# Attention and a mixture of experts on one core: joins and id copies on VectorE, earlier jump hints, a bank for the last tile, row stores one by one

## The chip, the core and the metric

The kernel runs on one core of one Trainium2 chip. The core has five engines that run side by side, each with an instruction stream of its own: TensorE (PE in the profile; its weight loads are PEld), VectorE (DVE), ScalarE (ACT), GpSimd (POOL) and SyncE (SP, which only issues transfers). The metric is the device time of one execution in microseconds (us).

## The reference

Windowed attention (8 batches, 8 heads, 576 positions, head size 64; each position sees itself and the 63 before it) gives 4608 tokens of 512 numbers. Each token goes to one of 8 experts, the one with the largest gate logit:

```python
logits = x @ w_gate
e_idx = np.argmax(logits, axis=1)
...
gate_w = probs[np.arange(N), e_idx]
eom = 1.0 / (1.0 + np.exp(-(x @ w_output_gate)))
for e in range(E):
    mask = e_idx == e
    h = np.maximum(x[mask] @ w1[e], 0.0)
    ye = h @ w2[e]
    out[mask] = gate_w[mask, None] * eom[mask, e, None] * ye
```

Everything is in 32-bit floats; w1 is 512 x 1024 and w2 is 1024 x 512 for each expert.

## The kernel before, in words

**Attention.** The loop over `t` takes 36 tiles of 128 tokens. For each it computes scores, exponentials, transposes and the product with v, and GpSimd copies the result (`xb`) into a row tile `xr` (L278), split into upper and lower halves of each 32-bit word. Tokens are routed in groups of four tiles (`GROUPS`; the last three groups are smaller). `route_a` finds each token's expert and weight, `route_b` its row in the buffer `xs` in device memory, which has a region for each expert; then it stores the rows with one indirect transfer for each tile of the group, all at once (L391 to L394, GpSimd's queue). A row holds the 512 words, the token's id and its weight. `xr` has two buffers. Early rows of expert 0 (two tiles) are read back while attention still runs (`early`, from group 6 on) and go through `joined` and `split` at L544.

**Experts.** `load_tile` (L483, L484) reads 128 rows by a transposing transfer into `halves`, and their ids and weights into `info`; both are issued by SyncE. `joined` puts the words together again from the two halves: GpSimd copies the upper half (L489), VectorE the lower (L490). `split` makes two parts, `xhi` on ScalarE (L493) and the rest `xlo` on VectorE (L494), so that three fast matmuls stand for one of full precision. `prep` calls both for two or four tiles. `layer1` runs 8 blocks of 12 matmuls into three banks of `ps_1`; ScalarE and VectorE evict each block as `hhi` and `hlo` (L623, L624). `layer2` runs 24 matmuls for one tile of 128 tokens into a bank of `ps_y` (three banks), VectorE evicts it times the weight into `y` (L639), and GpSimd stores it row by row by its ids (L640). `layer2_half` does a tile with at most 64 tokens; for it, GpSimd moves part of `hlo` into `hhi` (L627).

While an expert's layer 1 runs, `piece` splits the weights of the next one: ScalarE copies the upper part (L109), VectorE and GpSimd subtract (L110), and ScalarE's queue issues the load of a later piece into the `raw` buffer that has come free (L97).

**Order.** How many tokens an expert has is known only at run time. A Switch (L756) with 26 arms for each expert jumps to the code that fits: one pass of up to 512 columns, or one of 256 or 512 and a last one. All five engines jump. Each reads the number of the arm from memory into a register (`held`, L571) and gets a hint (`switch_hint`), so that the code of the arm is fetched ahead. Before, load and hint for the next expert stand after the arms (L779, L780), ahead of the last tile, `layer2(ws, 1, last)` (L781). As the program is built, each arm begins with a hint to its own end. A pass goes `masked` or a copy of the ids (L744), loads for the next pass, `layer1`, `prep`, then layer-2 tiles 2, 3 and 0; tile 1 comes last. In the section of the experts the order of TensorE, ScalarE and VectorE is as written (`manual_schedule`, L711); the order of GpSimd's and SyncE's instructions, and of all engines in the attention loop, is chosen by the compiler's scheduler. The data give experts 0, 1, 3 and 5 one pass and experts 2, 4, 6 and 7 two.

Of the kernel before, what the change touches and what calls it, by code (L numbers as in the profile page):

```python
# [19 lines left out]
P = 128  # L20
# [3 lines left out]
DM = H * D  # L24
# [16 lines left out]
def attn_moe(ctx: ExitStack, tc: tile.TileContext, qT, kT, vp, wg, w1, w2, out):  # L41
# [78 lines left out]
    ac = pool(rest, "ac", 1)  # L120
    erow = ac.tile([P, 8, 2 * P], U16, name="erow")
    nc.gpsimd.memset(erow, 0)
    xbp, xrp, xtp, gsp, sm = pool(rest, "xbp", 2), pool(rest, "xrp", 2), pool(rest, "xtp", 2), pool(rest, "gsp", 2), pool(rest, "sm", 4)
    ps_g = pool(rest, "ps_g", 1, space=PSUM)
    qsp, ktp, vpl = pool(big, "qsp", 3), pool(big, "ktp", 3), pool(big, "vpl", 3)
    pp, ptp = pool(big, "pp", 4), pool(big, "ptp", 2)
# [210 lines left out]
                                axis=AX.X, op=ALU.add)  # L337

    rts = {}

    def route_a(gi):

# [28 lines left out]
    def route_b(gi):  # L371

        G, (lg, _), xr = GROUPS[gi], bank_of(gi), xrs[gi]
        ohb, wm, ssum = rts.pop(gi)
        rk = lg[:, :, 2 * NE:3 * NE]
        for j in range(G):
            nc.tensor.matmul(rk[:, j], ones, ebase, start=True, stop=False)
            nc.tensor.matmul(rk[:, j], ones, csum_b, start=False, stop=False)
            for jj in range(j):
                nc.tensor.matmul(rk[:, j], ones, ohb[:, jj], start=False, stop=False)  # L380
            nc.tensor.matmul(rk[:, j], tri, ohb[:, j], start=False, stop=True)

        nc.vector.scalar_tensor_tensor(out=ssum, in0=wm, scalar=1.0, in1=ssum, op0=ALU.add, op1=ALU.mult)
        nc.vector.reciprocal(out=xr[:, 0:G, DM + 1:DM + 2].bitcast(F32), in_=ssum.unsqueeze(2))
        de = sm.tile([P, 4, NE], F32, name="de")[:, 0:G]
        nc.vector.tensor_tensor(out=de, in0=rk[:, 0:G], in1=ohb, op=ALU.mult)
        df = sm.tile([P, 4], F32, name="df")
        nc.vector.tensor_reduce(out=df[:, 0:G], in_=de, axis=AX.X, op=ALU.add)
        di = sm.tile([P, 4], I32, name="di")
        nc.vector.tensor_copy(out=di[:, 0:G], in_=df[:, 0:G])  # L390
        for j in range(G):  # L391
            ins = nc.gpsimd.indirect_dma_start(
                out=xs[:, :], out_offset=bass.IndirectOffsetOnAxis(ap=di[:, j:j + 1], axis=0),
                in_=xr[:, j, :], in_offset=None)  # L394

            tc.declare_no_dep(ins.ins, group="rows", reason="each token has a row of its own")
            tc.add_to_no_dep_group("rows", ins.ins)
        if gi == len(GROUPS) - 1:
            totals(ohb)
            return  # L400

        cs = sm.tile([P, NE], F32, name="cs")
        nc.vector.tensor_reduce(out=cs, in_=ohb.rearrange("p g e -> p e g"), axis=AX.X, op=ALU.add)
        nc.vector.tensor_tensor(out=csum, in0=csum, in1=cs, op=ALU.add)
        nc.vector.tensor_copy(out=csum_b, in_=csum)
# [80 lines left out]
    def joined(halves, x):  # L486

        words = x.bitcast(U16).rearrange("p k (n w) -> p k w n", w=2)
        nc.gpsimd.tensor_copy(out=words[:, :, 1], in_=halves[:, 0:KC])  # L489
        nc.vector.tensor_copy(out=words[:, :, 0], in_=halves[:, KC:2 * KC])  # L490

    def split(x, hi, lo):
        nc.scalar.copy(hi, x)  # L493
# [12 lines left out]
    for t in range(NT):  # L506
        if t + 4 < NT and t % 2 == 0:
            load_qk(t + 4)
            load_v(t + 4)
        if t % 3 == 1 and t // 3 < NPC:  # L510
            raws.append(load_piece(0, t // 3, nc.sync))
        if t % 3 == 0 and t > 0 and t // 3 <= NPC:
            split_piece(wsets[0], t // 3 - 1, raws.pop(0), nc.gpsimd.tensor_copy, (nc.gpsimd, nc.gpsimd))
        if 28 <= t < 26 + NRAW:
            load_piece(1, t - 28, nc.sync)
        if t < NT:
            ptrans(t)
        if t + 1 < NT:
            expo(t + 1, 0)
        for args in pend_s:  # L520
            gate_sum(*args)
        if t + 2 < NT:
            scores(t + 2)
        for gi in pend_b:
            route_b(gi)
            if gi == EARLY:
                early()
        pend_b = []
        for gi, gj, _ in pend_s:
            if gj + 2 == GROUPS[gi]:  # L530
                route_a(gi)
                pend_b.append(gi)
        pend_s = []
        if 1 <= t <= NT:
            xtrans(t - 1)
        if t >= NT - 2:
            i = t - (NT - 2)
            if i == 0:
                ehi = wst.tile([P, KC, 2 * P], F32R, name=f"raw{NRAW - 2}")
                elo = wst.tile([P, KC, 2 * P], F32R, name=f"raw{NRAW - 1}")  # L540
            cs = slice(i * P, (i + 1) * P)
            xe = xbp.tile([P, DM], F32, name="xb")
            xe = xe.rearrange("p (k n) -> p k n", k=KC)
            joined(erow[:, :, cs], xe)  # L544
            split(xe, ehi[:, :, cs], elo[:, :, cs])
        if t + 1 < NT:
            expo(t + 1, 1)
        if t < NT:
            pv(t)
        if 1 <= t <= NT:  # L550
            gi, gj = place[t - 1]
            if GROUPS[gi] < 4:
                gate_one(t - 1)
                if gj == GROUPS[gi] - 1:
                    route_a(gi)
                    pend_b.append(gi)
            elif gj % 2 == 1:
                pend_s.append(gate_pair(t - 1))
# [68 lines left out]
                nc.gpsimd.tensor_copy(out=hhi[f][:, half + 64:half + P], in_=hlo[f][:, half:half + 64])  # L627
            between(f)

    def layer2(ws, i, cur):  # L630
        yp = ps_y.tile([P, DM], F32, name="yp")
        cs = slice(i * P, (i + 1) * P)
        for f in range(FC):
            wh, wl = ws['h2'][f // 2][:, f % 2, :], ws['l2'][f // 2][:, f % 2, :]
            nc.tensor.matmul(yp, hhi[f][:, cs], wh, start=(f == 0), stop=False)  # L635
            nc.tensor.matmul(yp, hhi[f][:, cs], wl, start=False, stop=False)  # L636
            nc.tensor.matmul(yp, hlo[f][:, cs], wh, start=False, stop=(f == FC - 1))  # L637
        y = mo2.tile([P, DM], F32, name="y")
        nc.vector.tensor_scalar(out=y, in0=yp, scalar1=cur[:, i, 1:2], scalar2=None, op0=ALU.mult)  # L639
        nc.gpsimd.indirect_dma_start(out=out, out_offset=bass.IndirectOffsetOnAxis(ap=cur[:, i, 0:1].bitcast(I32), axis=0),  # L640
                                     in_=y, in_offset=None, bounds_check=N - 1, oob_is_err=False)
# [26 lines left out]
    with tc.manual_schedule(engines={ET.PE}):  # L668

        last_t, ws = NT - 1, wsets[0]  # L670
        cur0 = inf_p.tile([P, 4, 2], F32, name="cur")
        nc.gpsimd.tensor_copy(out=cur0[:, 0:2], in_=einfo)

        def early1(lo, hi):
            layer1(ws, 256, fr=range(lo, hi), xhi=ehi, xlo=elo)

        early1(0, 1)
        xtrans(last_t, ps_x, "tpx")
        early1(1, 2)
        for gi in pend_b:  # L680
            route_b(gi)
        gate_one(last_t)
        route_a(len(GROUPS) - 1)
        early1(2, 5)
        route_b(len(GROUPS) - 1)
        rest.close()
        wB = ctx.enter_context(tc.tile_pool(name="wB", bufs=1))
        wsets[1] = weight_set(wB, "b")
        off0 = nc.values_load(off_i[0:1, 0:1], engines=[ET.SP], min_val=0, max_val=256)
        ns0 = write_pads(0, off0)  # L690
        early1(5, FC)
        load_rows(places(0, 0))
        for j in range(NRAW - 2, NRAW):
            raw_t[j] = raw_tile(j)
        arm = held(arm_i, 0, 0, ARMS - 1)
        tc.switch_hint({g: arm for g in engs}, ARMS, "rows0")
        prep()
        layer2(ws, 0, cur0)
        layer2(ws, 1, cur0)
        for j in range(NRAW - 2, NRAW):  # L700
            load_piece(1, j, nc.sync)
# [9 lines left out]
    with tc.manual_schedule(engines={ET.PE, ET.Activation, ET.DVE}):  # L711
        for e in range(NE):
# [18 lines left out]
            def first_pass(cur, w, load, k=4):  # L731
# [4 lines left out]
                for i in (2, 3):  # L736
                    if w > i * P + 64:
                        layer2(ws, i, cur)
                    elif w > i * P:
                        layer2_half(ws, i, cur)  # L740
                layer2(ws, 0, cur)

            def next_pass(cur, w, load, k=4):
                nc.gpsimd.tensor_copy(out=cur, in_=info)  # L744
                load()
                layer1(ws, w)
                prep(k)
                for i in (2, 3, 0) if w == 512 else (0,):
                    layer2(ws, i, cur)

            def load_next():
                if more:
                    load_rows(first)

            last = inf_p.tile([P, 4, 2], F32, name="last")
            for a in tc.Switch(arm, ARMS, hint=f"rows{e}"):  # L756
                then, w = (0, 256 + a * STEP) if a <= NW else ((a - 1) // NW, 256 + ((a - 1) % NW + 1) * STEP)
                if then == 0:
                    first_pass(last, w, load_next, 4 if more else 0)
                else:  # L760
# [6 lines left out]
                    else:  # L767
# [7 lines left out]
                        if more:  # L775
                            load_rows(first)
                            prep()
            if more:
                arm = held(arm_i, e + 1, 0, ARMS - 1)  # L779
                tc.switch_hint({g: arm for g in engs}, ARMS, f"rows{e + 1}")  # L780
            layer2(ws, 1, last)  # L781


def _layout(q, k, v, gate_w, out_w):
# [38 lines left out]
```

## Time and profile before

| | |
|---|---|
| three timed runs | 683.36, 685.31, 690.81 us (median 685.31) |
| the profiled execution | 691.12 us, span 689.4 us |
| granted TensorE clock, mean | 0.96 of full |
| attention, up to the last tile's products | 0 to 212.8 us of the span, TensorE busy 189.8 |
| early rows, routing, totals | 212.8 to 243.45 us, TensorE busy 27.95 |
| experts 0 to 7 | 243.45 to 680.1 us; starts at 243.45, 291.43, 332.27, 404.90, 452.44, 512.62, 552.86, 611.15 |
| last eviction and stores | to 689.4 us |
| device memory | 74.03 MB read, 21.54 MB written |

A timeline row has start, duration, engine, line, operation, output and inputs, and in square brackets the idle time of the engine before it with what ended it; "issue" there means that nothing in the profile ended it. A row of waits has the total, the number and the longest. Rows of an engine with q, as POOLq or SPq, are those of its queue. q8 and q14 are queues that move instructions.

### The profile page before, as it was taken

How to read it: one execution, taken by the hardware profiler on the slowest of the kernel's cores; microseconds unless marked ns; L12 is line 12 of the kernel's file. 1: busy time of each engine (PE TensorE's matmuls, PEld its weight loads, DVE VectorE, ACT ScalarE, POOL GpSimd, SP SyncE). 2: the span in 40 equal slices, each digit the busy share in tenths (PEclk: the TensorE clock that was granted, in tenths of full speed). 3: DMA queues.
4: the chain of work that ended last, by engine and by line, in shares of the span. 5: the costliest groups of instructions: out<-in, count | busy, mean ns of one | idle time of the engine just before them, and what ended most of it. 6: DMA issues, size and time to landing. Idle time of an engine off the chain costs nothing. (4 is left out here: it accounts for less than half of the span.)

```text
span 689.4 us, 14987 instructions
## 1 busy us (share of the span) xinstructions
PE 629.1 (91%) x5271; PEld 522.1 (76%) x5271; DVE 352.4 (51%) x1266; ACT 266.4 (39%) x641; POOL 281.9 (41%) x348
## 2 busy tenths in 40 slices
PE   8998899899989898799999979989999989999994
PEld 5876577667669787697878868779989787978892
DVE  4796678777778545356261414426236445323120
ACT  4675567677662144062160215125126143212010
POOL 3467943453446246265182015327118348010101
PEclk9999789999997999999999999999999999999998
DMA  9899688777521557573552366265338464020100
GB/s 352 298 354 310 238 279 302 253 256 268 195 75 67 99 165 170 140 189 116 131 141 70 92 157 184 74 139 155 101 119 209 141 156 106 20 67 1 42 18 32
DMA packets 79324, 108.25 MB, mean 157 GB/s; under 512 B 54287, under 2 KB 54287, under 8 KB 76816
## 3 DMA queue, kind: packets, MB, share of 16 engines
q1 hardware_dynamic: 65552, 72.48, 36.2%
q0 software_dynamic: 5952, 18.92, 7.4%
q10 hardware_dynamic: 7616, 14.68, 6.9%
q8 instruction: 61, 1.00, 0.6%
q14 instruction: 143, 1.17, 0.6%
HBM read 74.03 MB, written 21.54 MB: 139 GB/s over the span
## 5 line engine op out<-in xcount | busy, mean ns | idle before, releaser
L623 ACT ACTIVATE hhi<-hp 128x256 fp32r<-128x256 f32 (+4 forms) x104 | 49.4, 475 | 268.3 <-PE hp L621 248.0
L225 ACT ACTIVATE pr<-pr,nmx 128x128 f32<-128x128 f32 x288 | 94.9, 394 | 46.2 <-DVE nmx L218 37.0
L624 DVE SCALAR_TENSOR_TENSOR hlo<-hp,hhi 128x256 fp32r<-128x256 f32 (+4 forms) x104 | 55.8, 536 | 106.8 <-ACT hhi L623 106.6
L621 PE MATMUL hp<-xhi,w1ha 128*128 128x256 f32 (+4 forms) x224 | 72.9, 325 | 7.6 <-DVE hlo L624 7.6
L640 POOL DMA_INDIRECT out_dram<-y,last x21 | 20.6, 979 | 141.2 <-POOLq L756 79.9
L621 PE MATMUL hp<-xlo,w1ha 128*128 128x256 f32 (+4 forms) x224 | 72.4, 323 | 0.7 <-DVE xlo L494 0.7
L621 PE MATMUL hp<-xhi,w1la 128*128 128x256 f32 (+4 forms) x224 | 72.4, 323 | 0.0
L635 PE MATMUL yp<-w2ha,hhi 128*128 128x512 f32 x160 | 63.8, 398 | 8.6 <-DVE y L639 4.3
L621 PE MATMUL hp<-xhi,w1hb 128*128 128x512 f32 (+2 forms) x160 | 58.0, 363 | 5.4 <-issue 5.4
L637 PE MATMUL yp<-w2ha,hlo 128*128 128x512 f32 x160 | 62.9, 393 | 0.0
L636 PE MATMUL yp<-w2la,hhi 128*128 128x512 f32 x160 | 62.8, 393 | 0.0
L278 POOL COPY xr<-xb 128x512 uint16<-128x512 uint16 x72 | 41.8, 614 | 49.2 <-DVE xb L272 49.0
L218 DVE CUSTOM_DVE_ANT_0 pr<-sp,m_int 128x128 f32<-128x128 f32 x224 | 49.5, 285 | 19.7 <-PE tp L289 9.5
L266 PE MATMUL o<-v,pt 128*64 128x65 f32 x1152 | 51.3, 237 | 8.3 <-issue 7.9
L621 PE MATMUL hp<-xlo,w1hb 128*128 128x512 f32 (+2 forms) x160 | 57.5, 360 | 0.0
L621 PE MATMUL hp<-xhi,w1lb 128*128 128x512 f32 (+2 forms) x160 | 57.2, 358 | 0.0
L211 PE MATMUL sp<-kt,q 64*64 64x128 f32 x1152 | 52.7, 296 | 4.6 <-issue 2.1
L266 PEld LDWEIGHTS o<-v,pt 128*64 128x64 f32 x1152 | 43.0, 148 | 18.1 <-issue 15.1
L635 PE MATMUL yp<-w2hb,hhi 128*128 128x512 f32 x128 | 51.2, 400 | 3.9 <-DVE y L639 3.9
L639 DVE TENSOR_SCALAR y<-yp,last 128x512 f32<-128x512 f32 x21 | 15.7, 750 | 72.1 <-PE yp L637 46.6
L621 PEld LDWEIGHTS hp<-xhi,w1ha 128*128 128x128 f32 x224 | 43.7, 195 | 10.6 <-DVE hlo L624 8.9
L211 PEld LDWEIGHTS sp<-kt,q 64*64 64x64 f32 x1152 | 39.8, 145 | 14.9 <-issue 11.9
(192 smaller groups left out, 1373.4 us busy)
## 6 DMA issues: line engine op xcount, KB each, us to landing
v<-in_vp_dram SPq DMA_DIRECT2D x18, 1040.0 KB, 7.3
raw<-in_w_dram SPq DMA_DIRECT2D x36, 512.0 KB, 4.4
raw<-in_w_dram ACTq DMA_DIRECT2D x28, 512.0 KB, 4.6
kt<-in_kT_dram SPq DMA_DIRECT2D x18, 640.0 KB, 7.6
q<-in_qT_dram SPq DMA_DIRECT2D x18, 512.0 KB, 6.1
xs<-padt SPq DMA_DIRECT2D x8, 257.0 KB, 5.5
halves<-xs SPq DMA_TRANSPOSE x40, 3.4
info<-xs SPq DMA_DIRECT2D x40, 1.0 KB, 2.1
```

Of the source, the lines that this page charges most:

```text
L211: nc.tensor.matmul(sps[ab][qb, hp, :], q[ds, t % 2, hp, qb], kt[ds, hp, k0:k0 + P], start=True, stop=True, tile_position=(ab * 64, blk * 64))
L218: nc.vector.tensor_tensor_reduce(out=pr[:, u, :], in0=sps[ab][:, hp, :], in1=m, scale=-0.125, scalar=3.0e38, op0=ALU.add, op1=ALU.min, acc ...
L225: nc.scalar.activation(out=pr[:, u, :], in_=pr[:, u, :], func=AF.Exp, bias=nmx[:, u:u + 1], scale=-1.0)
L266: nc.tensor.matmul(o[blk * 64:blk * 64 + 64, h // 4, c0:c0 + 65], pt[:, u, blk * 64:blk * 64 + 64], v[:, t % 2, blk, h, :], start=True, st ...
L278: nc.gpsimd.tensor_copy(out=xr[:, w], in_=xh[:, 1 - w])
L621: nc.tensor.matmul(hp_[:, 0:n], ws[wi][k][:, fs], xi[:, k, 0:n], start=(k == 0 and first), stop=(k == KC - 1 and last))
L623: nc.scalar.activation(out=hhi[f][:, cs], in_=hp_[:, 0:n], func=AF.Relu)
L624: nc.vector.scalar_tensor_tensor(out=hlo[f][:, cs], in0=hp_[:, 0:n], scalar=0.0, in1=hhi[f][:, cs].bitcast(F32), op0=ALU.max, op1=ALU.subt ...
L635: nc.tensor.matmul(yp, hhi[f][:, cs], wh, start=(f == 0), stop=False)
L636: nc.tensor.matmul(yp, hhi[f][:, cs], wl, start=False, stop=False)
L637: nc.tensor.matmul(yp, hlo[f][:, cs], wh, start=False, stop=(f == FC - 1))
L640: nc.gpsimd.indirect_dma_start(out=out, out_offset=bass.IndirectOffsetOnAxis(ap=cur[:, i, 0:1].bitcast(I32), axis=0), in_=y, in_offset=Non ...
```

## The change

The upper half of `joined` moves from GpSimd to VectorE, and so does the id copy at the head of a later pass. The jump hint moves from after the arms to inside each arm, ahead of the pass's layer-2 tile 0, two tiles ahead of the jump; the register load for it moves one expert earlier still, so two loads stand ahead of the first arm. The last tile of each expert gets the bank of `ps_x`, used until then only once, ahead of the experts. The row stores of groups 0 to 4 are put on a list and issued one at each step of the attention loop; from group 5 on they are issued at once as before. `xr` gets a third buffer, `gs` loses its second.

```diff
-    ... pool(rest, "xrp", 2), pool(rest, "xtp", 2), pool(rest, "gsp", 2), pool(rest, "sm", 4)
+    ... pool(rest, "xrp", 3), pool(rest, "xtp", 2), pool(rest, "gsp", 1), pool(rest, "sm", 4)
...
+    stores = []
+    def store():
+        xr, di, j = stores.pop(0)
+        ins = nc.gpsimd.indirect_dma_start(
+            out=xs[:, :], out_offset=bass.IndirectOffsetOnAxis(ap=di[:, j:j + 1], axis=0),
+            in_=xr[:, j, :], in_offset=None)
...
-        for j in range(G):
-            ins = nc.gpsimd.indirect_dma_start(
...
+        stores.extend((xr, di, j) for j in range(G))
+        if gi >= EARLY - 1:
+            while stores:
+                store()
...
-        nc.gpsimd.tensor_copy(out=words[:, :, 1], in_=halves[:, 0:KC])
-        nc.vector.tensor_copy(out=words[:, :, 0], in_=halves[:, KC:2 * KC])
+        for w in range(2):
+            nc.vector.tensor_copy(out=words[:, :, w], in_=halves[:, (1 - w) * KC:(2 - w) * KC])
...
+        if stores:
+            store()
         if t < NT:
             ptrans(t)
...
-    def layer2(ws, i, cur):
-        yp = ps_y.tile([P, DM], F32, name="yp")
+    def layer2(ws, i, cur, ps=ps_y, nm="yp"):
+        yp = ps.tile([P, DM], F32, name=nm)
...
-        arm = held(arm_i, 0, 0, ARMS - 1)
-        tc.switch_hint({g: arm for g in engs}, ARMS, "rows0")
+        arms = [held(arm_i, e, 0, ARMS - 1) for e in range(2)]
+        def jump_soon(e):
+            if e < NE:
+                tc.switch_hint({g: arms[e] for g in engs}, ARMS, f"rows{e}")
+        jump_soon(0)
...
                         layer2_half(ws, i, cur)
+                if cur is last:
+                    jump_soon(e + 1)
                 layer2(ws, 0, cur)
...
-                nc.gpsimd.tensor_copy(out=cur, in_=info)
+                nc.vector.tensor_copy(out=cur, in_=info)
                 load()
                 layer1(ws, w)
                 prep(k)
-                for i in (2, 3, 0) if w == 512 else (0,):
+                for i in (2, 3) if w == 512 else ():
                     layer2(ws, i, cur)
+                if cur is last and k:
+                    jump_soon(e + 1)
+                layer2(ws, 0, cur)
...
-            for a in tc.Switch(arm, ARMS, hint=f"rows{e}"):
+            for a in tc.Switch(arms[e], ARMS, hint=f"rows{e}"):
...
                             load_rows(first)
                             prep()
+                            jump_soon(e + 1)
-            if more:
-                arm = held(arm_i, e + 1, 0, ARMS - 1)
-                tc.switch_hint({g: arm for g in engs}, ARMS, f"rows{e + 1}")
-            layer2(ws, 1, last)
+            if e + 2 < NE:
+                arms.append(held(arm_i, e + 2, 0, ARMS - 1))
+            layer2(ws, 1, last, ps_x, "tpx")
```

More of the change, by code (lines that the diff above doesn't have):

```diff
@@ L122, in attn_moe @@
     nc.gpsimd.memset(erow, 0)
-    xbp, xrp, xtp, gsp, sm = pool(rest, "xbp", 2), pool(rest, "xrp", 2), pool(rest, "xtp", 2), pool(rest, "gsp", 2), pool(rest, "sm", 4)
+    xbp, xrp, xtp, gsp, sm = pool(rest, "xbp", 2), pool(rest, "xrp", 3), pool(rest, "xtp", 2), pool(rest, "gsp", 1), pool(rest, "sm", 4)
     ps_g = pool(rest, "ps_g", 1, space=PSUM)
@@ L339, in attn_moe @@
     rts = {}
+    stores = []
[4 more added lines that the diff above has]
+            in_=xr[:, j, :], in_offset=None)
+        tc.declare_no_dep(ins.ins, group="rows", reason="each token has a row of its own")
+        tc.add_to_no_dep_group("rows", ins.ins)
     def route_a(gi):
@@ L390, in route_b @@
         nc.vector.tensor_copy(out=di[:, 0:G], in_=df[:, 0:G])
-        for j in range(G):
-            ins = nc.gpsimd.indirect_dma_start(
[L393 to L397, printed above, removed]
+        stores.extend((xr, di, j) for j in range(G))
+        if gi >= EARLY - 1:
+            while stores:
+                store()
         if gi == len(GROUPS) - 1:
```

## The prediction

> **What bounds the kernel now.** I read the page first, then TensorE's list of waits, then its timeline around each wait.
>
> ```profile
> PE 629.1 (91%) x5271; PEld 522.1 (76%) x5271; DVE 352.4 (51%) x1266; ACT 266.4 (39%) x641; POOL 281.9 (41%) x348
> ```
>
> TensorE is busy for 91% of the span and no other engine for more than 51%. So time comes only out of the stretches in which TensorE stands still, or runs at a lower clock after one. Its waits (total us, times, longest):
>
> ```profile
> PE yp L635 <- DVE y L639: 8.2, 8, 1.7
> PE hp L621 <- DVE hlo L624: 7.6, 4, 3.0
> PE hp L621 <- issue: 5.4, 2, 3.7
> PE yp L635 <- DVE tab_i L440: 2.4, 1, 2.4
> ```
>
> Three of them belong to three of the four edits: eight waits of the last tile for VectorE, the layer-1 waits for VectorE's hlo, and two waits for nothing that the profile shows. No row of this list names GpSimd's row stores.
>
> **Own bank for the last tile.** The pass of expert 2 that ends at 401 us, and the entry to expert 4:
>
> ```profile
> 394.70 0.75 DVE L639 TENSOR_SCALAR y<-yp,last 128x512 f32<-128x512 f32 x1 [0.37 <-PE yp L637]
> 395.51 0.50 PE L635 MATMUL yp<-w2ha,hhi 128*128 128x512 f32 x1 [0.84 <-DVE y L639]
> 404.90 0.76 PE L621 MATMUL hp<-xhi,w1hb 128*128 128x512 f32 x1 [3.65 <-issue]
> 452.44 0.32 PE L621 MATMUL hp<-xhi,w1ha 128*128 128x352 f32 x1
> 455.80 0.23 DVE L706 TENSOR_SCALAR msk<-rowi,r_f 128x4 int32<-128x4 f32 x1 [2.40 <-issue]
> ```
>
> Tile 1 starts 0.06 us after the eviction of tile 0 ends (394.70 + 0.75), so it waits for that eviction, although it has a bank of its own among three. The reason is the join of the Switch: arms use the banks in different order, so the first matmul after them waits for the last eviction of whichever arm ran. A tile in the ps_x pool was last read by the last tile of the expert before, long done, so the wait goes: up to 8.2 us. hhi and hlo of that tile are also written in the arms, but ahead of the preparation and the evictions there, so waiting for them costs nothing. What stays between arm and tile is the register load for a jump (six times of eight, now two experts ahead). In the kernel before it hides under the wait, so it costs at most 0.84 each, 6 x 0.84 = 5.0, at least 0. I take 0.1 each: at 452.44 TensorE entered a new arm with no idle time while VectorE idled 2.40 us for the same jump, so TensorE's instruction stream runs at least about that far ahead of its array. Gain 7.5, bounds 3.2 and 8.2.
>
> **Hints two tiles ahead.** The other total, 5.4 us in two waits, is the entry to experts 1 and 3 (1.74 and 3.65). Which code arrives when can be read from the instruction queues. First the SyncE row, then queue parts of the windows 392.5 to 401.5, 401.5 to 403.5 and, for the good entry to expert 5, 503.5 to 507.5:
>
> ```profile
> 394.48 1.38 SPq L94 DMA_DIRECT2D raw<-in_w_dram  x2
> q14 instruction: 6, 0.05, 1.7%
> q8 instruction: 1, 0.02, 3.2%
> q8 instruction: 1, 0.02, 1.8%
> ```
>
> In the bad case the 16 KB block (I take q8 for TensorE's queue: the bad entry follows its packet) doesn't move in the nine microseconds in which the two weight loads of 394.48 move; it comes at 401.5 to 403.5 and TensorE starts at 404.90. In the good case it has come before 507.5. So the hint, given at the join, stands behind 1 MB of weights. Given one tile earlier (a tile takes 404.90 - 3.65 - 395.51 = 5.7 us, so at about 389.8 instead of 395.5) it goes ahead of them. With the slow clock behind the longer wait (the two windows of 404 and 408 below: 4 x (0.41 + 0.02) = 1.7) the whole is 7.1. I take 5.5, since one late block may remain; bounds 7.1 and, if the edit does harm, the third rival.
>
> **Id copies in program order.** Expert 4 has two passes; the copy of line 744 belongs to the second but stands early in GpSimd's queue, and there it waits for its ids. Timeline rows, then the windows' rows (the third figure from the right is the granted clock):
>
> ```profile
> 462.29 0.19 POOL L744 COPY last<-info 128x8 f32<-128x8 f32 x1 [6.95 <-DMA info<-xs]
> 462.44 2.48 POOL L110 TENSOR_TENSOR w1lb<-raw,w1hb 128x512 fp32r<-128x512 f32 x2
> 464.19 0.46 ACT L623 ACTIVATE hhi<-hp 128x352 fp32r<-128x352 f32 x1 [6.13 <-POOL w1lb L110]
> 465.27 0.43 PE L621 MATMUL hp<-xhi,w1ha 128*128 128x352 f32 x1 [3.00 <-DVE hlo L624]
> 347.46 0.50 PE L621 MATMUL hp<-xhi,w1ha 128*128 128x512 f32 x1 [1.42 <-DVE hlo L624]
> 564.26 0.42 PE L621 MATMUL hp<-xhi,w1ha 128*128 128x320 f32 x1 [2.44 <-DVE hlo L624]
> ```
>
> ```profile
> 404.00:408.00 4.00, 3.10 (x7) 2.48 (x8) 0.47 (x3) 0.00 (x0) 0.00 (x0) 0.59 0.69 145
> 408.00:412.00 4.00, 4.00 (x18) 3.25 (x17) 1.29 (x2) 1.63 (x3) 0.70 (x1) 0.98 0.72 127
> 464.00:468.00 4.00, 2.73 (x12) 2.73 (x13) 2.77 (x4) 3.32 (x8) 3.06 (x3) 0.77 0.64 204
> 468.00:472.00 4.00, 4.00 (x22) 4.00 (x21) 3.13 (x6) 3.58 (x9) 3.35 (x3) 0.80 0.86 279
> 564.00:568.00 4.00, 3.74 (x17) 3.74 (x18) 3.33 (x6) 3.45 (x8) 3.91 (x5) 0.65 0.84 229
> 568.00:572.00 4.00, 4.00 (x25) 3.77 (x25) 3.24 (x5) 3.44 (x9) 4.00 (x6) 0.93 0.83 296
> ```
>
> The chain is: the copy holds GpSimd 6.95 us; the splits of line 110 come behind it; ScalarE's next weight load needs the raw buffer that the split still reads, and in ScalarE's order hhi stands behind that load; VectorE's hlo needs hhi; TensorE needs the bank that hlo frees. The same happens in experts 2 and 6: 1.42 + 3.00 + 2.44 = 6.9 us. The clock stays down for some microseconds after the two longer waits: 4 x (0.23 + 0.20) = 1.7 and 4 x (0.35 + 0.07) = 1.7. Together 10.3. On VectorE the copy stands behind the first pass, when its ids have long come. What the move adds is a later release of the id tile: SyncE's next id loads now wait for VectorE.
>
> ```profile
> 344.60 1.98 SPq L484 DMA_DIRECT2D info<-xs  x4
> 360.06 2.67 SPq L483 DMA_TRANSPOSE halves<-xs  x2
> 378.75 0.98 POOL L640 DMA_INDIRECT out_dram<-y,cur  x1 [3.91 <-DVE y L639]
> 390.05 1.39 DVE L490 COPY raw<-halves 128x1024 uint16<-128x1024 uint16 x2
> halves<-xs SPq DMA_TRANSPOSE x40, 3.4
> ```
>
> In expert 2 these loads went out at 344.60; now they wait for the eviction ahead of 378.75. If the row loads of 360.06 stand behind them in SyncE's queue, the rows land at about 378.0 + 1.98 + 2.67 + 3.4 = 386.1, and are joined at 390.05: hidden, with 4 us left; without that cover the cost would be 8 us in each of three experts. I take 9.0, as GpSimd stays nearly full in expert 6; bounds 5.0 and 10.3.
>
> [...]
>
> **Joins on VectorE.** By shape, and two waits of TensorE:
>
> ```profile
> L489 POOL COPY raw<-halves 128x1024 uint16<-128x1024 uint16 x20 | 33.0, 1652 | 24.6 <-DMA halves<-xs 23.7
> L490 DVE COPY raw<-halves 128x1024 uint16<-128x1024 uint16 x20 | 22.5, 1148 | 7.8 <-DMA halves<-xs 3.9 <-POOL w2la L110 2.5 <-POOL w2lb L110 1.3
> 576.32 0.50 PE L651 MATMUL yp<-w2ha,hhi 128*128 128x512 f32 x1 [1.53 <-POOL hhi L627]
> 244.62 0.45 PE L621 MATMUL hp<-xlo,w1ha 128*128 128x416 f32 x1 [0.74 <-DVE xlo L494]
> ```
>
> 20 copies of 1.65 us leave GpSimd; VectorE does 40, which alone take 0.70 (1.39 for two at 390.05), so 28 instead of 22.5 us. Two for the early rows, of half the size, move too. VectorE's extra falls at the end of layer 1, with one to four layer-2 tiles of 5.7 us before xlo is wanted: hidden; queued behind it are only evictions, which the last tile no longer awaits. Uncovered it would be 5.5 us. GpSimd, freed, gets to the cast of 576.32 earlier (1.53), and at 244.62 two short copies replace the long one (at most 0.74). I take a gain of 1.0, bounds 0 and 2.3.
>
> **Row stores and the two early register loads.** The count of stores stays 36; from group 0 to 4 they go out one per tile, so a third xr buffer is needed.
>
> ```profile
> POOL xr L257 <- DMA xs<-xr,di: 24.0, 8, 5.3
> 229.60 0.17 DVE L437 TENSOR_SCALAR arm_i<-tot 128x8 int32<-128x8 f32 x1
> 230.99 0.79 PE L635 MATMUL yp<-w2ha,hhi 128*128 128x512 f32 x1 [2.44 <-DVE tab_i L440]
> ```
>
> GpSimd's 24 us go, but TensorE doesn't wait for GpSimd in that phase: 0. As all other engines are placed anew around it, bounds are plus and minus 2, the size of a TensorE wait like the 2.44 here. Ahead of the first arm a second register load comes onto TensorE's path; the first, with its hint, took at most 230.99 - 229.77 = 1.2. I take 0.3 more, bounds 0 and 1.2; the 0.74 of 244.62 covers much of it.
>
> **The sum.** -7.5 - 5.5 - 9.0 - 1.0 + 0 + 0.3 = -22.7 us. The profiled execution took 691.1 (span 689.4 and 1.7 around it): 668.4. Against the median shown, 685.3, that is 16.9 less, 2.5%: the profiled one is the longest seen, and I think late code blocks are what differs, which the changed kernel should not have. With the best bounds, 691.1 - 8.2 - 7.1 - 10.3 - 2.3 - 2 = 661.2; with the worst inside this forecast, 691.1 - 3.2 - 5.0 + 2 + 1.2 = 686.1.
>
> **Rivals.**
> 1. The last tile still waits at the join (0 instead of 7.5), for something else that is written in the arm. For it: the wait is a join's, not a bank's own. Against: only evictions and preparation follow the writes of hlo. 675.9.
> 2. The hint does nothing early: an engine fetches the target only when it is near its jump, or the weights still go ahead. For it: fetches stood behind weights. The 5.5 stays: 673.9.
> 3. Slower: the jump out of the arm. Each arm of the Switch begins with a hint to its own end. If an engine keeps one hint, the new one, given inside the arm, displaces that, and TensorE waits at seven joins for the block of the end. Price: a late block as at 404.90, 3.65 + 1.7 = 5.35 each. With the two late entries still there: 673.9 + 7 x 5.35 = 711.4. It decides from (685.3 - 673.9)/7 = 1.6 us a join. Against: the stream ran at least 2.4 us ahead at 452.44, and ahead of the join stands a whole tile with no wait in it. [...] No run here shows a jump without a hint.
>
> **How the numbers follow.** Forecast 0.62, rival 1 0.10, rival 2 0.12, rival 3 0.08, and 0.08 for mishaps of a few us. About 1% is what a measurement of this kernel can tell from no change: faster is below 678.5, slower above 692.2. Faster: 0.60 + 0.07 + 0.10 + 0.03 = 0.80; same: 0.02 + 0.03 + 0.02 + 0.02 + 0.03 = 0.12; slower: 0.06 + 0.02 = 0.08. The range runs from the best bound, 661, to 685, through the first two rivals and to the start of no gain; about 0.17 is outside.
>
> **What would show it.** Right: no wait of L635 for L639 in TensorE's list; no issue waits at L621; the three layer-1 waits of 347, 465 and 564 gone, with the clock at 1.00 behind them; L489 gone from GpSimd. Rival 1: eight waits of about 0.8 at the last tile. Rival 3: issue waits of TensorE ahead of the last tile of experts 0 to 6. Wrong altogether: new waits of TensorE for xlo (rows late through SyncE), or a longer attention phase than before.

## The result and the profile after

The changed kernel takes 662.82 us (median; 656.39 to 664.69), the kernel before beside it 687.72 us (683.36 to 690.81). The ratio is 0.9626, interval 0.9535 to 0.9716: faster. A second comparison, in the third set of experiments below, gave 658.33 against 677.24 us, ratio 0.9697, interval 0.9641 to 0.9754. Medians and ranges are of all executions of a kernel; the ratios and their intervals leave out those more than 1.5% longer than its shortest, which are seven of twelve for the ids alone, five of twelve for the joins alone and four of six for the hint given twice, the profiled one among them each time.

The forecast of 668.4 stood against a profiled execution of 691.1, a ratio of 0.9672, which lies in both intervals. Against the median 685.3, which the prediction names too, it is 0.9753: outside the first interval and at the edge of the second.

The profiled execution after took 662.07 us, span 660.3. Its first row, and TensorE's list of waits from the end of the early phase on (total us, times, longest):

```profile
PE 618.2 (94%) x5271; PEld 517.0 (78%) x5271; DVE 359.6 (54%) x1292; ACT 266.2 (40%) x641; POOL 246.6 (37%) x322
```

```profile
PE hp L631 <- DVE hlo L634: 2.4, 3, 1.1
PE hp L631 <- issue: 2.4, 1, 2.4
PE yp L645 <- ACT hhi L633: 1.2, 1, 1.2
PE tpx L645 <- issue: 1.1, 1, 1.1
PE yp L661 <- POOL hhi L637: 0.9, 1, 0.9
```

(L631 is L621 of before, L645 is L635, L649 is L639.) These five add up to 8.0 us. The same stretch of before had 8.2 for the eviction, 7.6 for hlo, 5.4 at the entries, 1.9 for hhi, 1.5 for GpSimd's hhi and 0.7 for xlo: 25.3. The eviction wait is gone altogether; of the layer-1 waits a third is left; of the two late entries one is left, at another expert; and one new wait stands at a join. The timeline has the places: TensorE's first layer-2 tile, the join of expert 0 and the entry to expert 5, and VectorE's entry to expert 1:

```profile
226.26 0.78 PE L645 MATMUL yp<-w2ha,hhi 128*128 128x512 f32 x1 [2.84 <-DVE tot L486]
275.38 0.47 PE L645 MATMUL tpx<-w2ha,hhi 128*128 128x512 f32 x1 [1.09 <-issue]
488.63 0.66 PE L631 MATMUL hp<-xhi,w1hb 128*128 128x416 f32 x1 [2.38 <-issue]
```

```profile
283.74 0.75 DVE L649 TENSOR_SCALAR y<-tpx,last 128x512 f32<-128x512 f32 x1 [7.49 <-DMA xs<-xr,di]
284.59 0.23 DVE L720 TENSOR_SCALAR msk<-rowi,r_f 128x4 int32<-128x4 f32 x1
```

VectorE starts the new arm 0.10 us after its last eviction. Before, it stood still for 2.40 us ahead of the new arm at the entry to expert 4, which the prediction shows. Over all entries:

```profile
DVE msk L720 <- issue: 5.2, 5, 1.9
```

The same row of before is the next one, so the earlier hint does bring the code earlier on VectorE too:

```profile
DVE msk L706 <- issue: 20.1, 7, 3.9
```

**Where the time came from.** The span is 29.1 us shorter. Up to the first layer-2 tile it is 230.99 - 226.26 = 4.7 us; behind it (689.4 - 230.99) - (660.3 - 226.26) = 24.4. Of the 24.4, 25.3 - 8.0 = 17.3 are waits; the rest is TensorE's own time (busy 423.8 us of this stretch before and 416.8 after, at a mean granted clock of 0.98 and 0.99), which was longer in the slow clock behind waits. The prediction had 22.7 for this stretch and 0 for the one ahead of it. So in this pair of profiles its sum is right within 1.7 us where it argued, and the other 4.7 came from a phase in which it expected nothing. In the second pair, below, the same stretch gains 28.1 us, 5.4 more than the sum.

### The profile page after: what moved, and what is told of

The parts are those of the page before. It is cut to its first block, busy times and chain, and to the rows that moved or that the text cites. A ratio compares the mean times of both kernels' runs of the same rounds, so it can differ in the third digit from the quotient of the medians.

```text
span 660.3 us, 15012 instructions
## 1 busy us (share of the span) xinstructions
PE 618.2 (94%) x5271; PEld 517.0 (78%) x5271; DVE 359.6 (54%) x1292; ACT 266.2 (40%) x641; POOL 246.6 (37%) x322
## 5 line engine op out<-in xcount | busy, mean ns | idle before, releaser
L631 PE MATMUL hp<-xhi,w1ha 128*128 128x256 f32 (+4 forms) x224 | 71.3, 318 | 1.7 <-DVE hlo L634 1.7
L631 PE MATMUL hp<-xlo,w1ha 128*128 128x256 f32 (+4 forms) x224 | 71.1, 317 | 0.0
L631 PE MATMUL hp<-xhi,w1la 128*128 128x256 f32 (+4 forms) x224 | 71.0, 317 | 0.0
L631 PE MATMUL hp<-xhi,w1hb 128*128 128x512 f32 (+2 forms) x160 | 57.8, 361 | 3.1 <-issue 2.4
L631 PE MATMUL hp<-xlo,w1hb 128*128 128x512 f32 (+2 forms) x160 | 57.8, 361 | 0.0
L631 PE MATMUL hp<-xhi,w1lb 128*128 128x512 f32 (+2 forms) x160 | 57.3, 358 | 0.0
L645 PE MATMUL yp<-w2ha,hhi 128*128 128x512 f32 x128 | 50.7, 396 | 4.1 <-DVE tot L486 2.8
L266 PE MATMUL o<-v,pt 128*64 128x65 f32 x1152 | 48.4, 235 | 4.3 <-issue 4.2
L211 PEld LDWEIGHTS sp<-kt,q 64*64 64x64 f32 x1152 | 37.9, 137 | 17.3 <-issue 13.1
L266 PEld LDWEIGHTS o<-v,pt 128*64 128x64 f32 x1152 | 41.5, 146 | 12.3 <-issue 10.6
L647 PE MATMUL yp<-w2ha,hlo 128*128 128x512 f32 x128 | 50.4, 393 | 0.0
L646 PE MATMUL yp<-w2la,hhi 128*128 128x512 f32 x128 | 50.3, 393 | 0.0
L650 POOL DMA_INDIRECT out_dram<-y,cur x15 | 14.8, 984 | 92.1 <-DVE y L649 71.5
L631 PEld LDWEIGHTS hp<-xhi,w1ha 128*128 128x128 f32 x224 | 42.4, 190 | 3.8 <-DVE hlo L634 2.3
L345 POOL DMA_INDIRECT xs<-xr,di x36 | 35.5, 987 | 25.8 <-DVE xb L272 9.8
```

The lines of the kernel that those rows point to most:

```text
L211: nc.tensor.matmul(sps[ab][qb, hp, :], q[ds, t % 2, hp, qb], kt[ds, hp, k0:k0 + P], start=True, stop=True, tile_position=(ab * 64, blk * 64))
L266: nc.tensor.matmul(o[blk * 64:blk * 64 + 64, h // 4, c0:c0 + 65], pt[:, u, blk * 64:blk * 64 + 64], v[:, t % 2, blk, h, :], start=True, st ...
L345: ins = nc.gpsimd.indirect_dma_start(out=xs[:, :], out_offset=bass.IndirectOffsetOnAxis(ap=di[:, j:j + 1], axis=0), in_=xr[:, j, :], in_of ...
L631: nc.tensor.matmul(hp_[:, 0:n], ws[wi][k][:, fs], xi[:, k, 0:n], start=(k == 0 and first), stop=(k == KC - 1 and last))
```

## The experiments

The theory is the prediction's: four waits of TensorE among the experts go, each by its own part, and the row stores do nothing. Its rivals are that a part brings nothing by itself, since another wait takes the place of the one removed; that the 4.7 us ahead of the experts belong to the row stores; and that a hint given early costs at the join.

Ratios are to the kernel before on the same chip; a set has one chip.

### Each part alone (first set: bank, hints, ids, stores; the kernel before 691.08 us)

**The bank alone.**

```diff
-            layer2(ws, 1, last)
+            layer2(ws, 1, last, ps_x, "tpx")
```

> The kernel before with the own bank for the last tile alone. My theory (the eight waits of the last tile for the eviction of tile 0 are waits for a bank): 7 to 8 us less than before, ratio 0.988 to 0.990, and no wait of the last tile for the eviction in TensorE's list; the register load and the hint that stand ahead of that tile stay hidden. Rival (the wait is for something else written in the arm): ratio 1.00 and eight waits of about 0.8 us.

684.53 us, ratio 0.9922 (0.9876 to 0.9968), which is 5.4 us (2.2 to 8.6). TensorE's waits:

```profile
PE hp L621 <- DVE hlo L624: 9.5, 6, 2.5
PE hp L621 <- issue: 6.9, 4, 2.6
PE hp L621 <- DMA out_dram<-y,last: 1.9, 1, 1.9
```

No wait for the eviction stands in the list, so the wait was the bank's. But code is late at four entries for 6.9 us, against two and 5.4 before, and a fifth entry waits 1.9 us. The other profiles bear this out. In the five that have the hint at the join and the eviction wait (the kernel before twice, and the ids, the joins and the stores alone), the row of late entries has one or two for 2.5 to 5.4 us; in the two that have the hint at the join and no eviction wait (this one, and the whole change with the hint back at the join, below), four and five for 6.9 and 9.3 us. So the eviction wait had covered late code: whoever comes to the jump sooner waits there instead. That fits a gain of 5.4 from 8.2 us of waits, though the interval does not exclude 8.2.

**The hints alone.**

```diff
+                if cur is last:
+                    jump_soon(e + 1)
                 layer2(ws, 0, cur)
...
-            if more:
-                arm = held(arm_i, e + 1, 0, ARMS - 1)
-                tc.switch_hint({g: arm for g in engs}, ARMS, f"rows{e + 1}")
+            if e + 2 < NE:
+                arms.append(held(arm_i, e + 2, 0, ARMS - 1))
```

> The kernel before with the earlier hints alone (register loads two experts ahead, hint inside the arm, ahead of tile 0). My theory: the late code blocks at two of seven entries go, 3 to 7 us less, ratio 0.990 to 0.996, and VectorE's 2.4 to 3.9 us without a reason at seven entries shrink. Rival 2 (early hints do nothing): ratio 1.00, entries as before. Rival 3 (the hint to the arm's end is displaced and the join waits for its block): issue waits of TensorE ahead of the last tile, ratio above 1.00 if they are more than 1 us each.

677.94 us, ratio 0.9858 (0.9791 to 0.9925), 9.8 us (5.2 to 14.4): the largest middle value of the five.

```profile
PE yp L635 <- DVE y L639: 9.4, 8, 3.4
PE hp L621 <- DVE hlo L624: 2.5, 3, 1.4
PE hp L621 <- issue: 0.9, 1, 0.9
```

The entries fall from 5.4 to 0.9, as they should. The waits for hlo fall too, from 7.6 to 2.5, though GpSimd still copies the ids. A likely reason, not tested by itself, is that the other engines enter the arm earlier too, so that the ids are read earlier and the copy holds GpSimd for less time: its waits ahead of the copy come to 10.0 us in three here, 18.2 in three before.

**The id copies alone.**

```diff
-                nc.gpsimd.tensor_copy(out=cur, in_=info)
+                nc.vector.tensor_copy(out=cur, in_=info)
```

> The kernel before with the id copies on VectorE alone. My theory: the layer-1 waits of experts 2, 4 and 6 (1.42, 3.00, 2.44) go with the slow clock behind two of them: 8 to 10 us less, ratio 0.985 to 0.988. Rival (VectorE's copy holds back the next id and row loads): new waits for xlo at the entries, ratio 0.99 to 1.01.

685.88 us, ratio 0.9887 (0.9840 to 0.9935), 7.8 us (4.5 to 11.1).

```profile
PE yp L635 <- DVE y L639: 14.1, 8, 4.7
PE yp L651 <- POOL hhi L627: 3.8, 2, 2.7
PE hp L621 <- DVE hlo L624: 0.4, 1, 0.4
```

The chain through GpSimd is confirmed: of 7.6 us of waits for hlo 0.4 are left, with this one line changed. But as much comes back elsewhere, above all at the join, where the wait for the eviction is now 14.1: all of TensorE's waits from expert 0 on come to 25.8 us in this profile, against 25.3 before. So the profile does not show where a gain in time would come from, and its size is uncertain: by the medians of all executions it is 5.2 us. No wait for xlo was added, so the rows did not come late through SyncE's queue.

**The row stores alone.** With three `xr` buffers and one `gs`:

```diff
-        for j in range(G):
-            ins = nc.gpsimd.indirect_dma_start(
...
+        stores.extend((xr, di, j) for j in range(G))
+        if gi >= EARLY - 1:
+            while stores:
+                store()
...
+        if stores:
+            store()
         if t < NT:
             ptrans(t)
```

> The kernel before with the row stores one per tile alone (third xr buffer, one gs buffer). As predicted: 0, ratio 0.997 to 1.003, attention as long as before (212.8 us in the profile). Rival, after the changed kernel's profile, whose layer 1 begins 6.0 us earlier (206.8): the stores are the cause, 4 to 6 us less, ratio 0.991 to 0.994, with layer 1 beginning at about 207.

686.17 us, ratio 0.9961 (0.9918 to 1.0004): 2.7 us, with zero just inside. More on it below.

### The joins alone, and the change without one part (second set; before 681.38 us)

**The joins alone.**

```diff
-        nc.gpsimd.tensor_copy(out=words[:, :, 1], in_=halves[:, 0:KC])
-        nc.vector.tensor_copy(out=words[:, :, 0], in_=halves[:, KC:2 * KC])
+        for w in range(2):
+            nc.vector.tensor_copy(out=words[:, :, w], in_=halves[:, (1 - w) * KC:(2 - w) * KC])
```

> Both joined copies on VectorE alone, the rest as before. Prediction's term: a gain of 1.0 us (0 to 2.3), 690 us against 691, with the 0.74 wait for xlo at the early rows and the 1.53 wait at the last expert smaller. Rival: VectorE's 5.5 us more come onto the path at the layer-2 tiles that still wait for its evictions: waits of the last tile for VectorE rise from 8-10 to 12 us or more, and the kernel is 2 to 4 us slower. A third reading: no difference that can be measured, as the other three parts and the stores already sum to the whole change (0.8 + 1.4 + 1.1 + 0.4 per cent of 3.7).

675.68 us, ratio 0.9923 (0.9879 to 0.9967), 5.2 us (2.2 to 8.2). The rival, longer waits at the last tile, is not there (8.7 us):

```profile
PE yp L635 <- DVE y L639: 8.7, 8, 2.0
PE hp L621 <- DVE hlo L624: 6.3, 4, 2.9
PE hp L621 <- issue: 2.5, 2, 2.3
```

The gain is more than the predicted 1.0, and its place can't be read from this list: the wait for GpSimd's hhi at the half tile is gone (1.5 before, and 0.3 to 3.8 in the other kernels), and only one entry is late by more than 0.2. Both vary among the other runs as well. That 5.2 us is the joins' own is the reading of the times; by which wait stays open.

**The change with hint and register load back at the join.**

```diff
-                if cur is last:
-                    jump_soon(e + 1)
...
+            if more:
+                arm = held(arm_i, e + 1, 0, ARMS - 1)
+                tc.switch_hint({g: arm for g in engs}, ARMS, f"rows{e + 1}")
```

> The whole change with the hint and the register load back at the join. Theory: the hints are worth more than the 5.5 us predicted, since the other parts take away the waits under which late code had been hidden: about 673 us against 663, waits of TensorE for nothing that the profile shows at five or more of the entries, 7 to 12 us in all, and VectorE idle by 2.4 us or more at each entry. Rival: hints are worth only their own 5.5 us: 668, two late entries.

665.64 us, ratio 0.9779 (0.9688 to 0.9870).

```profile
PE hp L631 <- issue: 9.3, 5, 2.5
```

```profile
DVE msk L716 <- issue: 21.4, 7, 4.9
```

Five entries are late for 9.3 us in all, where the whole change has one of 2.4: 6.9 us by the waits. By the ratios it is 0.8 to 1.5% of 681 us (against 0.9697 and 0.9626), 6 to 10 us; the intervals overlap, so the waits are the better measure here. Behind the first layer-2 tile this profile takes 661.3 - 217.32 = 444.0 us, 10 more than the 434.0 of the whole change. Without the eviction waits, the hint at the join is late for five of seven entries. The two parts lean on each other: the bank uncovers the late code, and the earlier hint takes it away.

**The hint still earlier.**

```diff
                 load()
+                if cur is last:
+                    jump_soon(e + 1)
                 layer1(ws, w, piece, half=...)
```

(and no longer ahead of tile 0; the same in `next_pass`)

> The whole change with the hint still earlier, ahead of the last pass's layer 1 instead of behind its first layer-2 tiles. If the one late entry that is left (expert 5, 2.38 us and some 1.7 us of slow clock) is late because the weight loads still went ahead of the block, it goes, and the time is about 659 us; the joins stay without waits. The rival of the displaced hint: the arm's own exit hint, given at the arm's start, is now displaced for the whole pass, so the joins wait (1 to 3.7 us at several of seven joins), and the time is 670 us or more. If neither holds, 663 within 1.5.

659.45 us, ratio 0.9699 (0.9646 to 0.9752): by the time no different from the whole change. But its attention ended early in the profile (first layer-2 tile at 217.82), and behind that tile it takes 661.7 - 217.82 = 443.9 us, 10 more than the whole change. My theory fell: the late entry at expert 5 was not cured, it grew to 5.04 us, so the weight loads ahead of the block are not its reason.

```profile
PE hp L631 <- issue: 5.0, 1, 5.0
PE tpx L645 <- issue: 2.4, 4, 1.2
```

The second row is what the prediction's third rival names: TensorE waits at four joins for nothing that the profile shows, 0.22 to 1.23 us each, where the whole change has one such wait of 1.09 in its first profile and none in its second. So a hint given long before the join seems to cost at the join, by 0.6 us each, not 5.35.

**The change without the spread stores.** With two `xr` buffers and two `gs`:

```diff
-        stores.extend((xr, di, j) for j in range(G))
-        if gi >= EARLY - 1:
-            while stores:
-                store()
+        for j in range(G):
+            ins = nc.gpsimd.indirect_dma_start(
...
-        if stores:
-            store()
```

> The whole change without the spread row stores (stores of a group together again, two xr buffers). If the stores are what shortened attention, the time is about 667 us against 663, and the early rows' layer 1 starts at about 211 to 213 us instead of 206.8. Rival, the prediction's 0: the start of layer 1 differs from kernel to kernel only by how the other engines' instructions happen to be placed; the time stays within 1.5 us of 663.

657.48 us, ratio 0.9681 (0.9616 to 0.9746). The first layer-2 tile came at 219.15 us, earlier than the 226.26 of the whole change. This spoke against the theory that the stores shorten attention, but the whole change was not run on this chip, so the third set put them side by side.

### Side by side, and a hint given twice (third set; before 677.24 us)

**The whole change, the kernel before and the change without spread stores.**

> The changed kernel itself once more, beside the next two on one chip. Expected ratio to before 0.96 to 0.965. Two profiled executions with the same instructions on every engine up to the first expert's arms (this kernel and the one with the earlier hint) had their first layer-2 tile at 226.3 and at 217.8 us. If attention varies that much by itself, the start here can lie anywhere from 217 to 231; if the kernel set it, it is again near 226.

> The kernel before once more, for its profile on the same chip: its first layer-2 tile at 231.0 us in its first profile. If the row stores shorten attention, it is again 5 us or more later than that of the changed kernel here; if attention varies by itself, the two differ by less than that or the other way round. Its waits among the experts should repeat: the last tile for VectorE about 8 us in eight waits, id copies 6 to 9 us; the late entries (5.4 in two) may come at other experts.

> The change without the spread stores again, now beside the whole change. Theory after the first such run: the stores are worth 2 to 4 us (0.3 to 0.6 per cent), a ratio to before of 0.966 to 0.968 where the whole change has 0.962. The prediction's 0: the two kernels agree within 0.3 per cent.

The whole change: 658.33 us, 0.9697 (0.9641 to 0.9754). Without spread stores: 656.23 us, 0.9697 (0.9636 to 0.9757). So no difference is measured here, though the intervals leave room for some 4 us either way. And the end of attention moves without a change in the code. The first layer-2 tile of the kernel before, then of the whole change, each with the late entry that it has, then that tile in the kernel with the hint still earlier, whose instructions are the same as those of the whole change on every engine up to the first arms:

```profile
220.03 0.49 PE L635 MATMUL yp<-w2ha,hhi 128*128 128x512 f32 x1 [2.47 <-DVE tot L478]
393.90 0.47 PE L621 MATMUL hp<-xhi,w1hb 128*128 128x512 f32 x1 [3.23 <-issue]
```

```profile
224.32 0.79 PE L645 MATMUL yp<-w2ha,hhi 128*128 128x512 f32 x1 [2.84 <-DVE tot L486]
484.19 0.43 PE L631 MATMUL hp<-xhi,w1hb 128*128 128x416 f32 x1 [2.33 <-issue]
```

```profile
217.82 0.79 PE L645 MATMUL yp<-w2ha,hhi 128*128 128x512 f32 x1 [2.84 <-DVE tot L486]
```

The kernel before starts its first layer-2 tile at 230.99 in one profile and at 220.03 in another; the whole change's code starts it at 226.26, 224.32 and 217.82. These profiles come from different sets, so how much of the difference belongs to the chip is not known; within this set the same code has 224.32 here and 226.68 in the kernel with the hint given again. In this set the change has the longer attention, by 4.3 us, and is still faster; the prediction had named a longer attention as a sign that it was wrong altogether, and that sign can't be trusted. What is behind the first layer-2 tile repeats: 681.3 - 220.03 = 461.3 before (458.4 in the first profile), 657.5 - 224.32 = 433.2 after (434.0), a gain of 28.1. The waits of that stretch, before and after:

```profile
PE hp L621 <- DVE hlo L624: 10.8, 5, 3.2
PE yp L635 <- DVE y L639: 9.5, 8, 3.4
PE hp L621 <- issue: 3.2, 1, 3.2
PE yp L651 <- POOL hhi L627: 2.7, 1, 2.7
```

```profile
PE yp L661 <- POOL hhi L637: 3.8, 2, 2.8
PE hp L631 <- issue: 2.3, 1, 2.3
PE hp L631 <- DVE hlo L634: 1.1, 2, 0.9
```

A difference between the sets can be named, though not explained. In the first 200 us the kernel before has such a row in its first profile, and the stores alone, in the first set, the one behind it:

```profile
PE o L266 <- issue: 7.9, 13, 1.1
```

```profile
PE o L266 <- issue: 3.7, 8, 1.1
```

The bank, the hints and the ids alone have 7.0 to 8.0 there, the whole change 4.2 in its first profile. In the second and third set it is at most 0.7, with stores spread or not. So where TensorE has these waits, the two kernels with spread stores have some 4 us less of them, which fits 2.7 us in the first set; what the waits are for was not found. In the second and third set TensorE waits for VectorE's `xb` instead (L289 for L272): 8.9 to 14.5 us in the four profiles with spread stores, 16.0 to 20.2 in the four without. Those waits are shorter with spread stores too, and still no time is gained in the third set; why is open.

**The hint given again behind the join.**

```diff
             if e + 2 < NE:
                 arms.append(held(arm_i, e + 2, 0, ARMS - 1))
+            jump_soon(e + 1)
             layer2(ws, 1, last, ps_x, "tpx")
```

> The whole change with the hint for the next jump given a second time, behind the join. Theory: the entry to expert 5 (2.38 us, 5.04 with the earlier hint) is late because the block that the hint brought is lost again when the arm's own end and the code behind it are fetched; given again, the hint brings it back only after the end's code, at the same time as in the kernel before, so the entry wait shrinks or goes and the time is 2 to 4 us shorter (ratio about 0.957). Rival: the block was never asked for in time because of the weight loads, or the second hint stands behind them: no change, 0.962 within 0.003. A third reading, the second hint costs: six more issues on every engine behind the join, waits of TensorE at the joins of 0.2 to 1 us each, 0.965 or more.

653.27 us (643.20 to 657.04), the lowest median of all: 5.1 us less than the whole change by the medians of six executions each, whose ranges overlap (653.26 to 661.19 there). The ratio, 0.9540 (0.9457 to 0.9623), lies below the interval of the whole change but rests on two executions, 643.20 and 649.51, so that the gain in time is likely and its size is not settled. Behind the first layer-2 tile the profiled execution takes 655.3 - 226.68 = 428.6 us, 4.6 less than the 433.2 of the whole change. Its waits there hold no late entry and no wait at a join:

```profile
PE hp L631 <- DVE hlo L634: 2.4, 2, 1.5
PE yp L645 <- ACT hhi L633: 1.6, 1, 1.6
PE yp L661 <- POOL hhi L637: 1.1, 2, 0.9
```

The late entry to expert 5 stands in all four profiles that have the bank and the hint ahead of tile 0 alone (2.38 and 2.33 us in the whole change, 2.78 and 2.36 without the spread stores), so that its absence here is hardly chance. The instruction queues show that entry. First the whole change: a block for TensorE (q8) at 473.5 to 474.0, none in 474 to 481, and one more at 481.0 to 481.5, when the last tile's last matmul of 481.48 is at hand; the arm starts at 484.19.

```profile
q8 instruction: 1, 0.02, 18.9%
q14 instruction: 3, 0.02, 1.1%
q8 instruction: 1, 0.02, 14.1%
```

With the second hint a block comes at 478.0 to 478.5, as far ahead of the last tile as the 473.5 there, and then none until the jump (478.5 to 486.4 has only q14); the arm starts at 486.47 with no idle time.

```profile
q8 instruction: 1, 0.02, 17.5%
q14 instruction: 4, 0.03, 1.1%
```

So the whole change needs one block more, which comes as the last tile ends, and the second hint saves it. The theory on record expected the lost block to be brought a second time; no such block is seen. What is seen fits a target which the hint in the arm had brought, and which is given up at the join unless the hint is repeated. It doesn't prove it: the second hint adds instructions, and which code a block holds was not shown. A hint of another arm given at that place, with the same instructions, would tell the two apart; it was not tried. Nor is all of the 5.1 us this entry, which is 2.3: the wait for GpSimd's hhi at the half tile is also 2.7 us smaller (3.8 against 1.1), the waits for hlo and for ScalarE's hhi are 1.3 and 1.1 larger, and nothing ties these to the hint.

## Why the prediction was right

**The bank.** Right in mechanism: the join's wait was for the eviction of whichever arm ran, and with a bank of its own it went whole, 8.2 to 0 where 7.5 was taken (8.2 - 6 x 0.1 is 7.6). Its cover was misjudged. The step said that only the register load hides under the wait, at most 0.84 each. Late code was hidden there as well: alone, the bank gives 5.4 us, with four late entries instead of two.

**The hints.** Right that an earlier hint takes away late entries; the size was probably too small: 5.5 was taken from the two entries late in one profile. In the changed kernel, without the cover above, five entries would be late for 9.3 us; 2.4 is left, so 6.9 us, and as the first part alone the hint brings 9.8 (5.2 to 14.4). The reason given, that the hint must go ahead of 1 MB of weights, is not shown, and the traces speak against it. In the kernel before, the same two loads go out 1.0 us ahead of tile 1 at the late entry to expert 3 (394.48, the tile at 395.51) and at the good one to expert 5 (505.99, the tile at 507.01), where the block comes at 506.5 to 507.0 all the same. In the changed kernel two blocks come ahead of the loads both at the good entry to expert 3 (376 to 379 us, loads at 382.24) and at the late one to expert 5 (474 to 479 us, loads at 481.35); and with the hint given earlier, that entry grew from 2.3 to 5.0 us. The loads and the block at the good entry of before, then the loads at the two entries of the changed kernel:

```profile
505.99 1.37 SPq L94 DMA_DIRECT2D raw<-in_w_dram  x2
q8 instruction: 1, 0.02, 14.7%
382.24 0.99 SPq L94 DMA_DIRECT2D raw<-in_w_dram  x2
481.35 0.99 SPq L94 DMA_DIRECT2D raw<-in_w_dram  x2
```

The late entry to expert 3 is in both profiles of the kernel before (3.65 and 3.23), the one to expert 5 in both of the changed kernel. So they seem to go with the code of the arm; what in it makes them late is open.

**The id copies.** Right in mechanism: with the one line changed the waits for hlo went from 7.6 to 0.4. The size, 9.0, is not settled: 7.8 was measured alone (4.5 to 11.1; 5.2 by all medians), and in that profile as much wait came back elsewhere. In the changed kernel, of the three waits that the prediction names, only the last leaves a rest, 1.08 us, and that in the first profile alone. The cover of 4 us for the rows behind the later id loads held: no wait for xlo.

**The joins.** Mis-sized: 1.0 was taken with 2.3 as the bound, and alone they gave 5.2 (2.2 to 8.2, so that the interval just reaches the bound). The bound came from the two waits of TensorE that named GpSimd or its copy in one profile.

**The row stores.** Taken at 0, plus or minus 2. The interval alone is -0.3 to 5.7 us, and with the rest of the change the third set shows no difference. The 4.7 us less of attention in the first pair of profiles is not evidence: between sets the same code differs by 8 us there, and the kernel before by 11.

**The singles and the sum.** Alone the five give 5.4 + 9.8 + 7.8 + 5.2 + 2.7 = 30.9 us; together 20.5 (third set) to 25.7 (first comparison). The intervals of the singles are 3 to 5 us wide to each side, so that the times alone do not prove an overlap; the waits do, as the bank's gain is in part eaten by late code. The prediction's sum, 22.7, lies between the two in part by luck: the terms that it took too small (hints, joins) and the overlap that it left out offset each other. Against the medians, the forecast was 16.9 us less; measured were 687.72 - 662.82 = 24.9 and 677.24 - 658.33 = 18.9.

**The rivals.** The last tile's wait did not take another form (the first), and the hint is no empty one (the second: VectorE's idle time at the entries fell from 20.1 to 5.2). The third, the exit jump, has its wait in the traces, with 1.09 at one of seven joins, but not its price of 5.35 at each. At the entry to expert 5, in the second profile of the whole change, a block comes only as the last tile ends (481.0 to 481.5) and TensorE waits 2.33 us; at the six other entries TensorE does not wait. Whether one hint displaces another was not shown.

**The spread of the times.** The prediction thought late code blocks are what differs from run to run. That fell: the changed kernel, with one late entry, spreads over 8.3 us in four runs (656.39 to 664.69), the kernel before over 7.5. The end of attention moves by more than this between profiles (8.4 us for the whole change's code, 11.0 for the kernel before).

## What to carry to other kernels

A wait that stands ahead of a jump may hide late code (here two late entries of 5.4 us became four of 6.9 when 8.2 us of waits went); take the two away together, and price the second by what the first has covered, not by what it shows now. When one phase of a profile changes without a reason in the edit, profile the old kernel again before giving the edit credit. Where a hint is given well ahead of a jump and another jump lies between, it is worth trying to give it again behind that one (here 5.1 us less by the medians, whose ranges overlap).

## What was not expected of the hardware

The length of a wait did not tell here whether TensorE's clock falls behind it. The granted clock (third figure from the right) after 2.38 us in the whole change, at 488.63, and after 2.33 at the same place in its second profile:

```profile
488.00:492.00 4.00, 3.37 (x10) 3.28 (x11) 1.22 (x4) 0.00 (x0) 0.98 (x1) 0.58 0.40 90
```

```profile
484.00:488.00 4.00, 3.81 (x20) 3.73 (x21) 1.81 (x6) 1.14 (x3) 0.98 (x1) 1.00 0.55 116
```

And in the kernel before, after 1.86 us (wait for hhi at 270.29, first profile) and after 3.23 (393.90, second profile):

```profile
270.00:274.00 4.00, 3.71 (x10) 2.34 (x11) 3.27 (x4) 1.66 (x4) 3.94 (x4) 0.70 0.11 36
```

```profile
395.00:397.00 2.00, 2.00 (x10) 1.61 (x9) 0.22 (x2) 0.00 (x0) 0.00 (x0) 1.00 0.74 209
```

So the clock fell after 1.86 us of one place (to 0.70) and not after 3.23 of another (1.00), and at one and the same place it fell in one profile (0.58) and not in the other (1.00). What decides it was not shown. For the prediction this means that its 1.7 us of slow clock behind each long wait is a chance, not a fixed price.
